# Out-projection of a squared-relu feed-forward as seven block products in place of eight

## The chip, the cores and the metric

The kernel runs on one core of one Trainium2 chip. The metric is the device time of one execution in microseconds (us), and the median over the executions is quoted. All comparisons below use executions of the fast state, unless the text says otherwise. The engines are called TensorE (PE in the profile; PEld is its weight load), VectorE (DVE), ScalarE (ACT), GpSimd (POOL) and SyncE (SP).

## The reference

Sliding-window causal attention (window 64) over 8 batches of 8 heads, 576 positions and 64 columns, then a feed-forward layer with a squared relu over the 4608 tokens. Cut to what matters:

```python
def _attn_ref(q, k, v):                        # (8, 8, 576, 64) each
    scores = np.matmul(q, k.transpose(0, 1, 3, 2)) / np.sqrt(D)
    mask = (rel >= 0) & (rel < 64)             # rel = query position - key position
    ...                                        # softmax over the masked scores
    return np.matmul(attn, v)

def _moe_ref(x, w_in, w_out):                  # (4608, 512), (512, 2048), (2048, 512)
    h = np.maximum(x @ w_in, 0.0)
    return (h * h @ w_out).astype(np.float32)
```

## The kernel before

The 4608 tokens are nine groups of 512. For a group, the attention makes `xT`; the up-projection makes `h2 = relu(x @ w_in)^2` in fp16, 16 slices of 128 features; the out-projection multiplies `h2` by `w_out`. Groups 0 and 1 are special: there the data arrive while the attention is still being computed, so the up-projection goes in chunks of 128 tokens (matmuls of 128 columns). From group 2 on the up-projection uses matmuls of 512 columns and is woven together with the out-projection of the group before and the attention of the group after. A list scheduler fixes the final order of each engine's queue when the kernel is built; where the timelines below show a VectorE op held up, the ops behind it are late as well (e9: one copy of 2.46 us, and the three ops behind it end with it).

The parts that the change touches, and those that the argument needs:

```python
    wst = ctx.enter_context(tc.tile_pool(name="wst", bufs=4))
    stage = ctx.enter_context(tc.tile_pool(name="stage", bufs=15))
    st16 = ctx.enter_context(tc.tile_pool(name="st16", bufs=8))
    hrp = ctx.enter_context(tc.tile_pool(name="hrp", bufs=4))
    opool = ctx.enter_context(tc.tile_pool(name="opool", bufs=4))
    ps_up = ctx.enter_context(tc.tile_pool(name="ps_up", bufs=2, space=bass.MemoryType.PSUM))
    ps_out = ctx.enter_context(tc.tile_pool(name="ps_out", bufs=2, space=bass.MemoryType.PSUM))
    # ... cut ...
    def load_w_out():
        def one(f):
            ws = wst.tile([P, DM], FP32, name="ws2", tag="ws")
            nc.sync.dma_start(out=ws[:], in_=moe_w_out[f * P:(f + 1) * P, :])
            nc.gpsimd.tensor_copy(out=w_out_sb[:, f, :], in_=ws[:])      # fp32 -> fp16 cast

        return [lambda f=f: one(f) for f in range(FFC)]

    def load(i):                       # 128 tokens of k, q, v: DMA, then casts on GpSimd
        # ... cut ...
        nc.gpsimd.tensor_copy(out=k16s[i][:], in_=sts[0][:].rearrange("p h d -> p (h d)"))
        nc.gpsimd.tensor_copy(out=q16s[i][:], in_=sts[1][:].rearrange("p h d -> p (h d)"))
        # ... cut: the same for v, three copies ...

    def scores(i):
        # ... cut: 16 small matmuls, exp on ScalarE ...
            nc.vector.tensor_tensor(out=pm[:], in0=pm[:], in1=mask, op=ALU.min)   # the mask op

    def ffn_up_chunk(i):               # groups 0 and 1
        def one(fq):
            # ... cut: 16 matmuls of 128 columns into one PSUM bank hps ...
            hrelu = hrp.tile([P, 4, P], FP32, name="hrelu4", tag="hrelu")
            nc.scalar.activation(out=hrelu[:], in_=hps[:], func=AF.Relu)
            nc.vector.scalar_tensor_tensor(
                out=h2s[g][:, 4 * fq:4 * fq + 4, t0:t0 + P], in0=hps[:], scalar=0.0,
                in1=hrelu[:], op0=ALU.max, op1=ALU.mult)                # the squared-relu op

    def ffn_out(g):
        hold = {}

        def one(ts, fq):
            if fq == 0:
                hold["ps"] = ps_out.tile([P, DM], FP32, name="ops", tag="ps_o")
            for f in range(4 * fq, 4 * fq + 4):
                nc.tensor.matmul(
                    hold["ps"][:], h2s[g][:, f, ts * P:(ts + 1) * P], w_out_sb[:, f, :],
                    start=(f == 0), stop=(f == FFC - 1))
            if fq == 3:
                osb = opool.tile([P, DM], FP32, name="osb", tag="osb")
                nc.scalar.activation(out=osb[:], in_=hold["ps"][:], func=AF.Copy,
                                     scale=OUT_SCALE)
                # ... cut: DMA of osb to out ...
    # ... cut ...
    for g in range(1, NTB + 1):
        streams = [(ffn_out(g - 1), 0.0, 1.0)]
        if g >= 2 and g < NTB:
            streams.append((ffn_up(g), 0.0, 1.0))
        if g + 1 < NTB:
            streams.append((attention(g + 1), 0.0, 0.85))
        if g + 2 < NTB:
            streams.append((loads(g + 2), 0.0, 1.0))
        for s in weave(*streams):
            s()
```

The softmax here doesn't subtract the row's maximum and nothing guards it: scores larger than these inputs give would overflow.

Of the kernel before, what the change touches and what calls it, by code (L numbers as in the profile page):

```python
# [9 lines left out]
FP32 = mybir.dt.float32  # L10
FP16 = mybir.dt.float16
AF = mybir.ActivationFunctionType
ALU = mybir.AluOpType
# [14 lines left out]
def kernel(  # L28
# [21 lines left out]
    FFC = DFF // P  # L50
    NTB = NT // 512

    const = ctx.enter_context(tc.tile_pool(name="const", bufs=1))
    wst = ctx.enter_context(tc.tile_pool(name="wst", bufs=4))
    stage = ctx.enter_context(tc.tile_pool(name="stage", bufs=15))
    st16 = ctx.enter_context(tc.tile_pool(name="st16", bufs=8))
    attw = ctx.enter_context(tc.tile_pool(name="attw", bufs=3))
    smallp = ctx.enter_context(tc.tile_pool(name="smallp", bufs=4))
    xtp = ctx.enter_context(tc.tile_pool(name="xtp", bufs=3))
    h2pool = ctx.enter_context(tc.tile_pool(name="h2pool", bufs=2))  # L60
    hrp = ctx.enter_context(tc.tile_pool(name="hrp", bufs=4))
    opool = ctx.enter_context(tc.tile_pool(name="opool", bufs=4))
    ps_up = ctx.enter_context(tc.tile_pool(name="ps_up", bufs=2, space=bass.MemoryType.PSUM))
# [45 lines left out]
    def load_w_in():  # L109
# [14 lines left out]
        return steps  # L124

    def load_w_out():
        def one(f):
            ws = wst.tile([P, DM], FP32, name="ws2", tag="ws")
            nc.sync.dma_start(out=ws[:], in_=moe_w_out[f * P:(f + 1) * P, :])
            nc.gpsimd.tensor_copy(out=w_out_sb[:, f, :], in_=ws[:])  # L130

        return [lambda f=f: one(f) for f in range(FFC)]

# [35 lines left out]
    def transposes(i):  # L169
# [10 lines left out]
        nc.vector.tensor_copy(out=kT[:, :, 64:192], in_=ps[:, 0])  # L180
        qT = attw.tile([P, HP, P], FP16, name="qT", tag="qT")
        nc.scalar.activation(out=qT[:], in_=ps[:, 1], func=AF.Copy, scale=1.0)
# [16 lines left out]
    def transpose_q_dma(i):  # L199
        qT = attw.tile([P, HP, P], FP16, name="qTd", tag="qTd", bufs=8)  # L200
        nc.sync.dma_start_transpose(out=qT[:], in_=q16s[i][:])
        qTs[i] = qT
# [49 lines left out]
    def attention(g):  # L252

        steps = []
        fns = (transposes_k, scores, values, to_xT_dma)
        for t in range(4 + len(fns) - 1):
# [5 lines left out]
    def loads(g):  # L262
        steps = []
        for i in range(4 * g, 4 * g + 4):
            steps.append(lambda i=i: load(i))
            if i > 4 * g:
                steps.append(lambda i=i - 1: transpose_q_dma(i))
        steps.append(lambda i=4 * g + 3: transpose_q_dma(i))
        return steps
# [49 lines left out]
    def ffn_out(g):  # L319
        hold = {}  # L320

        def one(ts, fq):
            if fq == 0:
                hold["ps"] = ps_out.tile([P, DM], FP32, name="ops", tag="ps_o")
            for f in range(4 * fq, 4 * fq + 4):
                nc.tensor.matmul(  # L326
                    hold["ps"][:], h2s[g][:, f, ts * P:(ts + 1) * P], w_out_sb[:, f, :],
                    start=(f == 0), stop=(f == FFC - 1))
            if fq == 3:
                osb = opool.tile([P, DM], FP32, name="osb", tag="osb")  # L330
                nc.scalar.activation(out=osb[:], in_=hold["ps"][:], func=AF.Copy,  # L331
                                     scale=OUT_SCALE)
                nc.sync.dma_start(
                    out=out[(g * 4 + ts) * P:(g * 4 + ts + 1) * P, :], in_=osb[:])

        return [lambda ts=ts, fq=fq: one(ts, fq) for ts in range(4) for fq in range(4)]

# [61 lines left out]
```

## Time and profile before

| | before |
|---|---|
| time, median of 3 (range) | 338.17 us (337.17 to 339.39) |
| span of the profiled execution, mean granted TensorE clock | 336.6 us, 0.984 |
| TensorE busy, VectorE busy, GpSimd busy | 314.3, 199.6, 123.2 us |
| end of the last 128-column up-projection | 75.9 us |
| start of the first 512-column up-projection (group 2) | 110.6 us |
| first matmuls of the out-projections of groups 2 to 8 | 120.8, 161.4, 194.6, 226.9, 259.1, 291.1, 318.7 us |

The two middle rows split the program into stages.

The busy time of each engine in two stretches of the kernel before (columns: stretch, length, then busy time and number of instructions of PE, PEld, DVE, ACT and POOL, granted clock, DMA share, GB/s):

```profile
48.00:76.00 28.00, 25.98 (x466) 22.55 (x464) 23.97 (x55) 16.16 (x30) 19.21 (x32) 1.00 1.03 236
...
226.80:259.00 32.20, 32.20 (x275) 15.32 (x273) 20.80 (x48) 15.92 (x28) 9.69 (x16) 1.00 0.52 125
```

The first is the end of the 128-column stage: TensorE 26.0 of 28, VectorE 24.0 of 28. The second is one full iteration of the steady stage: VectorE has 11 us of room in 32.

VectorE's timeline of the kernel before, from 55 us on (start, duration, engine, line, operation, tiles, shapes):

```profile
55.02 0.41 DVE L220 TENSOR_TENSOR pm_1061<-pm_1061,mask_inner 128x512 f16<-128x512 f16 x1
55.40 0.43 DVE L220 TENSOR_TENSOR pm_1064<-pm_1064,mask_inner 128x512 f16<-128x512 f16 x1
55.89 0.69 DVE L306 SCALAR_TENSOR_TENSOR h_1087<-hps_1147,hrelu_1164 128x512 f16<-128x512 f32 x1
```

Two masks and a squared-relu op follow each other within 1.6 us. TensorE's timeline of the kernel before at the two milestones (start, duration, engine, line, operation, tiles, shapes):

```profile
74.86 1.05 PE L301 MATMUL hps_1557<-xT,w_in_sb 128*128 128x128 f16 x16
...
110.61 1.68 PE L280 MATMUL hps<-xT,w_in_sb 128*128 128x512 f16 x7
```

### The profile page before, as it was taken

To read this page: it belongs to the slowest core of one execution; us is meant where nothing else is said; L and a number is where in the kernel's file an instruction comes from. 1 tells how busy PE (TensorE), PEld (TensorE's weight loads), DVE (VectorE), ACT (ScalarE), POOL (GpSimd) and SP (SyncE) were. 2 spreads that over 40 slices of the span, in tenths; PEclk is the share of its full clock that TensorE was granted. 3 is DMA by queue.
4 is the path that set the end of the run, shared out by engine and by line. 5 is a ranking of instruction groups with operands and counts; after the bars stand their busy time and mean duration, and the time that the engine had idled before them with its cause. 6 is when DMAs were issued, how large, how long until landed. Compare 5 with 4: busy or idle time off the path is not lost.

```text
span 336.6 us, 7505 instructions
## 1 busy us (share of the span) xinstructions
PE 314.3 (93%) x2922; PEld 166.6 (49%) x2922; DVE 199.6 (59%) x478; ACT 148.8 (44%) x261; POOL 123.2 (37%) x204
## 2 busy tenths in 40 slices
PE   1957989999999999999999999999999999999995
PEld 0345778884554444444444454444444444444442
DVE  2655888981466687765586478646764666443300
ACT  1123656642333645453454445445543544444411
POOL 5007797586543553553172356337300000000000
PEclk9995899999999999999999999999999999999999
DMA  7899998898977987987793799899622013100121
GB/s 210 248 250 205 207 257 228 246 221 166 217 176 194 238 202 176 247 175 160 177 214 84 178 237 192 142 225 217 137 66 78 33 50 69 38 33 31 40 86 62
DMA packets 152803, 53.97 MB, mean 160 GB/s; under 512 B 144064, under 2 KB 144064, under 8 KB 152768
## 3 DMA queue, kind: packets, MB, share of 16 engines
q1 hardware_dynamic: 152768, 53.50, 68.0%
q8 instruction: 23, 0.38, 0.5%
q14 instruction: 12, 0.10, 0.1%
HBM read 36.70 MB, written 9.44 MB: 137 GB/s over the span
## 4 chain that ended last, share of the span: by engine, by line
PE 78%; DVE 10%; DMA 5%; ACT 3%; issue 1%; SPq 1%; ACTq 0%
PE ops L326 37%; PE hps L280 27%; DMA ws<-in_moe_w_in_dram 5%; PE av L230 4%; PE qkT_ps L189 2%; DVE h_397 L306 1%; DVE h_1087 L306 1%; DVE w_in_sb L117 1%; DVE h_2013 L285 1%; SPq L151 1%; PE hps_639 L301 1%; ACT hrelu L284 1%; DVE x_sb L235 1%; PE hps_506 L301 0%; PE qkT_ps L173 0%
## 5 line engine op out<-in xcount | busy, mean ns | idle before, releaser
L280 PE MATMUL hps<-xT,w_in_sb 128*128 128x512 f16 x448 | 113.2, 379 | 0.9 <-DVE h_3020 L285 0.4
L284 ACT ACTIVATE hrelu<-hps 128x512 f32<-128x512 f32 x112 | 66.9, 597 | 93.6 <-PE hps L280 91.8
L280 PEld LDWEIGHTS <-w_in_sb 128*128 128x128 f16 x448 | 43.3, 98 | 52.4 <-issue 2.1
L301 PEld LDWEIGHTS <-w_in_sb 128*128 128x128 f16 x512 | 32.0, 101 | 7.5 <-issue 2.7
L331 ACT ACTIVATE osb<-ops 128x512 f32<-128x512 f32 x36 | 21.5, 598 | 31.5 <-PE ops L326 30.7
L235 DVE TENSOR_TENSOR x_sb<-av,rden 128x256 f16<-128x256 f32 x72 | 27.5, 415 | 0.1
L285 DVE SCALAR_TENSOR_TENSOR h_4970<-hps,hrelu 128x512 f16<-128x512 f32 x16 | 11.1, 692 | 16.6 <-ACT hrelu L284 16.6
L196 DVE COPY kT<-qkT_ps 128x512 f16<-128x512 f16 x28 | 11.8, 422 | 12.9 <-PE qkT_ps L189 12.8
L234 DVE RECIPROCAL rden<-av 128x4 f32<-128x4 f32 x72 | 10.8, 175 | 13.9 <-PE av L230 13.9
L210 PEld LDWEIGHTS <-kT 64*128 64x128 f16 x576 | 11.5, 96 | 14.7 <-issue 12.6
L326 PE MATMUL ops<-w_out_sb,h_2013 128*128 128x512 f16 x64 | 17.3, 380 | 0.0
L326 PE MATMUL ops<-w_out_sb,h_2515 128*128 128x512 f16 x64 | 16.7, 380 | 0.0
L285 DVE SCALAR_TENSOR_TENSOR h_4528<-hps,hrelu 128x512 f16<-128x512 f32 x16 | 11.1, 692 | 9.4 <-ACT hrelu L284 9.1
L326 PE MATMUL ops<-w_out_sb,h_3522 128*128 128x512 f16 x64 | 16.5, 380 | 0.0
L326 PE MATMUL ops<-w_out_sb,h_3020 128*128 128x512 f16 x64 | 16.5, 380 | 0.0
L326 PE MATMUL ops<-w_out_sb,h_4027 128*128 128x512 f16 x64 | 16.5, 380 | 0.0
L326 PE MATMUL ops<-w_out_sb,h_4528 128*128 128x512 f16 x64 | 16.4, 379 | 0.0
L285 DVE SCALAR_TENSOR_TENSOR h_2515<-hps,hrelu 128x512 f16<-128x512 f32 x16 | 11.0, 688 | 8.6 <-ACT hrelu L284 8.5
L285 DVE SCALAR_TENSOR_TENSOR h_4027<-hps,hrelu 128x512 f16<-128x512 f32 x16 | 11.1, 692 | 8.1 <-ACT hrelu L284 7.9
L285 DVE SCALAR_TENSOR_TENSOR h_3522<-hps,hrelu 128x512 f16<-128x512 f32 x16 | 11.0, 687 | 8.0 <-ACT hrelu L284 7.9
L326 PE MATMUL ops<-w_out_sb,h_1087 128*128 128x512 f16 x64 | 15.7, 380 | 0.0
L285 DVE SCALAR_TENSOR_TENSOR h_3020<-hps,hrelu 128x512 f16<-128x512 f32 x16 | 11.0, 690 | 7.9 <-ACT hrelu L284 7.8
(783 smaller groups left out, 578.1 us busy)
## 6 DMA issues: line engine op xcount, KB each, us to landing
out_dram<-osb SPq DMA_DIRECT2D x36, 256.0 KB, 2.6
k_st<-in_k_dram SPq DMA_DIRECT2D x32, 256.0 KB, 3.7
q_st<-in_q_dram SPq DMA_DIRECT2D x32, 256.0 KB, 4.0
v_st<-in_v_dram SPq DMA_DIRECT2D x32, 256.0 KB, 4.2
ws<-in_moe_w_in_dram SPq DMA_DIRECT2D x16, 256.0 KB, 4.1
k_st<-in_k_dram SPq DMA_DIRECT2D x8, 128.0 KB, 3.4
q_st<-in_q_dram SPq DMA_DIRECT2D x8, 128.0 KB, 3.1
v_st<-in_v_dram SPq DMA_DIRECT2D x8, 128.0 KB, 4.1
```

What stands on the lines that cost most here:

```text
L189: nc.tensor.transpose(out=ps[:, hp, :], in_=src[i][:, hp * P:(hp + 1) * P], identity=ident[:])
L196: nc.vector.tensor_copy(out=kT[:, :, 64:192], in_=ps[:])
L210: nc.tensor.matmul(sc[hh][:, hp, blk, :], kTs[i][r0:r0 + 64, hp, 64 * blk:64 * blk + P], qTs[i][r0:r0 + 64, hp, 64 * blk:64 * blk + 64], s ...
L230: nc.tensor.matmul(av[64 * blk:64 * blk + 64, h % 4, 0:65], pms[i][h % 2][:, h // 2, blk, :], vv[:, h, 0:65], start=True, stop=True)
L234: nc.vector.reciprocal(out=rden[:], in_=av[:, :, 64:65])
L235: nc.vector.tensor_tensor(out=x_sb[:, 4 * half:4 * half + 4, :], in0=av[:, :, 0:D], in1=rden[:].to_broadcast([P, 4, D]), op=ALU.mult)
L280: nc.tensor.matmul(hps[:], w_in_sb[:, c, f * P:(f + 1) * P], xT_of(g)[:, c, :], start=(c == 0), stop=(c == DMC - 1))
L284: nc.scalar.activation(out=hrelu[:], in_=hps[:], func=AF.Relu)
L285: nc.vector.scalar_tensor_tensor(out=h2s[g][:, f, :], in0=hps[:], scalar=0.0, in1=hrelu[:], op0=ALU.max, op1=ALU.mult)
L301: nc.tensor.matmul(hps[:, f, :], w_in_sb[:, c, (4 * fq + f) * P:(4 * fq + f + 1) * P], xT_of(g)[:, c, t0:t0 + P], start=(c == 0), stop=(c ...
L326: nc.tensor.matmul(hold["ps"][:], h2s[g][:, f, ts * P:(ts + 1) * P], w_out_sb[:, f, :], start=(f == 0), stop=(f == FFC - 1))
L331: nc.scalar.activation(out=osb[:], in_=hold["ps"][:], func=AF.Copy, scale=OUT_SCALE)
```

## The change

The out-projection of one group is a product of a 2x2-block matrix (tokens 0 to 255 and 256 to 511, features 0 to 1023 and 1024 to 2047) and a 2x2-block `w_out` (features, output columns). Strassen's form needs seven block products in place of eight, so the intent is to take an eighth of the out-projection off TensorE. It pays with four sums of `h2` blocks per group (fp16, on VectorE, in two halves each: eight ops of 1024 elements per partition), four sums of `w_out` blocks once (16 ops of 512 on GpSimd) and five sums of results per group on VectorE as they leave PSUM. To make room in memory several pools become smaller, and the transposes of q for group 2 move from DMA to TensorE.

```diff
+    GQD = 3
-    stage = ctx.enter_context(tc.tile_pool(name="stage", bufs=15))
-    st16 = ctx.enter_context(tc.tile_pool(name="st16", bufs=8))
+    stage = ctx.enter_context(tc.tile_pool(name="stage", bufs=9))
+    st16 = ctx.enter_context(tc.tile_pool(name="st16", bufs=6))
+    spool = ctx.enter_context(tc.tile_pool(name="spool", bufs=1))
-    hrp = ctx.enter_context(tc.tile_pool(name="hrp", bufs=4))
-    opool = ctx.enter_context(tc.tile_pool(name="opool", bufs=4))
+    hrp = ctx.enter_context(tc.tile_pool(name="hrp", bufs=3))
+    opool = ctx.enter_context(tc.tile_pool(name="opool", bufs=3))
     # ... cut; in load_w_out():
+        def sums(k0):
+            ks, kl = slice(k0, k0 + 2), slice(KH + k0, KH + k0 + 2)
+            b11, b12 = w_out_sb[:, ks, 0:NH], w_out_sb[:, ks, NH:DM]
+            b21, b22 = w_out_sb[:, kl, 0:NH], w_out_sb[:, kl, NH:DM]
+            tt = nc.gpsimd.tensor_tensor
+            tt(out=wb[1][:, ks], in0=b22, in1=b12, op=ALU.subtract)
+            tt(out=b12, in0=b12, in1=b11, op=ALU.subtract)
+            tt(out=wb[0][:, ks], in0=b22, in1=b12, op=ALU.subtract)
+            tt(out=wb[2][:, ks], in0=b21, in1=wb[0][:, ks], op=ALU.subtract)
+        steps = []
+        for k in range(KH):
+            steps += [lambda f=k: one(f), lambda f=KH + k: one(f)]
+            if k % 2 == 1:
+                steps.append(lambda k0=k - 1: sums(k0))
     # ... cut; in ffn_out(g), for the old body:
+        S = [spool.tile([P, KH, TH], FP16, name=f"hs{i}", tag=f"hs{i}") for i in range(4)]
+        def hsum(i, half):
+            ks = slice(half * KH // 2, (half + 1) * KH // 2)
+            x, y, op = ((A[1][0], A[1][1], ALU.add), (S[0], A[0][0], ALU.subtract),
+                        (A[0][0], A[1][0], ALU.subtract), (A[0][1], S[1], ALU.subtract))[i]
+            nc.vector.tensor_tensor(out=S[i][:, ks], in0=x[:, ks], in1=y[:, ks], op=op)
+        # ... cut: product() issues 16 matmuls of 256 columns per half; evac() empties a bank,
+        #     ScalarE for a plain copy, VectorE (scale, then add) where a sum is due
+        plan = [
+            ("A", A[0][0], W[0][0], True, (("A", "p1"),)),
+            ("B", S[1], wb[0], True, (("B", "u2", "p1"),)),
+            ("A", A[0][1], W[1][0], False, (("A", "osb", None, 0, 0),)),
+            ("C", S[0], W[0][1], True, (("C", "u4", "u2"),)),
+            ("D", S[2], wb[1], True, (("D", "osb", "u4", 1, 1),)),
+            ("C", S[3], W[1][1], False, (("C", "osb", "u2", 0, 1, True),)),
+            ("D", A[1][1], wb[2], False, (("D", "osb", "u2", 1, 0, True),)),
+        ]
+        before = {0: (0, 1), 2: (2,), 4: (3,)}
```

More of the change, by code (lines that the diff above doesn't have):

```diff
@@ L124, in load_w_in @@
         return steps
+    KH = FFC // 2
+    NH = DM // 2
+    wb = [const.tile([P, KH, NH], FP16, name=f"wb{i}") for i in range(3)]
     def load_w_out():
@@ L130, in one @@
             nc.gpsimd.tensor_copy(out=w_out_sb[:, f, :], in_=ws[:])
-        return [lambda f=f: one(f) for f in range(FFC)]
+        def sums(k0):
[12 more added lines that the diff above has]
+                steps.append(lambda k0=k - 1: sums(k0))
+        return steps
     xTs = {}
@@ L180, in transposes @@
         nc.vector.tensor_copy(out=kT[:, :, 64:192], in_=ps[:, 0])
-        qT = attw.tile([P, HP, P], FP16, name="qT", tag="qT")
+        qT = attw.tile([P, HP, P], FP16, name="qT", tag="qT", bufs=8)
         nc.scalar.activation(out=qT[:], in_=ps[:, 1], func=AF.Copy, scale=1.0)
@@ L199, in transpose_q_dma @@
     def transpose_q_dma(i):
-        qT = attw.tile([P, HP, P], FP16, name="qTd", tag="qTd", bufs=8)
+        qT = attw.tile([P, HP, P], FP16, name="qT", tag="qT", bufs=8)
         nc.sync.dma_start_transpose(out=qT[:], in_=q16s[i][:])
@@ L254, in attention @@
         steps = []
-        fns = (transposes_k, scores, values, to_xT_dma)
+        fns = (transposes_k if g >= GQD else transposes, scores, values, to_xT_dma)
         for t in range(4 + len(fns) - 1):
@@ L265, in loads @@
             steps.append(lambda i=i: load(i))
-            if i > 4 * g:
+            if g >= GQD and i > 4 * g:
                 steps.append(lambda i=i - 1: transpose_q_dma(i))
-        steps.append(lambda i=4 * g + 3: transpose_q_dma(i))
+        if g >= GQD:
+            steps.append(lambda i=4 * g + 3: transpose_q_dma(i))
         return steps
@@ L319, in ffn_out @@
     def ffn_out(g):
-        hold = {}
-        def one(ts, fq):
-            if fq == 0:
-                hold["ps"] = ps_out.tile([P, DM], FP32, name="ops", tag="ps_o")
-            for f in range(4 * fq, 4 * fq + 4):
-                nc.tensor.matmul(
-                    hold["ps"][:], h2s[g][:, f, ts * P:(ts + 1) * P], w_out_sb[:, f, :],
-                    start=(f == 0), stop=(f == FFC - 1))
-            if fq == 3:
-                osb = opool.tile([P, DM], FP32, name="osb", tag="osb")
-                nc.scalar.activation(out=osb[:], in_=hold["ps"][:], func=AF.Copy,
-                                     scale=OUT_SCALE)
-                nc.sync.dma_start(
-                    out=out[(g * 4 + ts) * P:(g * 4 + ts + 1) * P, :], in_=osb[:])
@@ L336, in ffn_out @@
-        return [lambda ts=ts, fq=fq: one(ts, fq) for ts in range(4) for fq in range(4)]
+        h2 = h2s[g]
+        TH = 256
+        top = (slice(0, TH), slice(0, KH)), (slice(0, TH), slice(KH, FFC))
+        bot = (slice(TH, 512), slice(0, KH)), (slice(TH, 512), slice(KH, FFC))
+        A = [[h2[:, ks, ts] for ts, ks in row] for row in (top, bot)]
+        S = [spool.tile([P, KH, TH], FP16, name=f"hs{i}", tag=f"hs{i}") for i in range(4)]
+        banks, sums, osb = {}, {}, {}
+        def hsum(i, half):
[3 more added lines that the diff above has]
+            nc.vector.tensor_tensor(out=S[i][:, ks], in0=x[:, ks], in1=y[:, ks], op=op)
@@ new lines, in product @@
+        def product(bank, a, w, half, first):
+            if first and half == 0:
+                banks[bank] = ps_out.tile([P, 2, NH], FP32, name=f"ops{bank}", tag="ps_o")
+            for k in range(half * KH // 2, (half + 1) * KH // 2):
+                for m in range(2):
+                    nc.tensor.matmul(
+                        banks[bank][:, m, :], a[:, k, m * P:(m + 1) * P], w[:, k],
+                        start=(first and k == 0 and m == 0), stop=(k == KH - 1),
+                        skip_group_check=True)
@@ new lines, in evac @@
+        def evac(bank, to, add=None, row=0, col=0, send=False):
+            if to == "osb":
+                if row not in osb:
+                    osb[row] = opool.tile([P, 2, DM], FP32, name="osb", tag="osb")
+                dst = osb[row][:, :, col * NH:(col + 1) * NH]
+            else:
+                sums[to] = wst.tile([P, 2, NH], FP32, name=to, tag="ws")
+                dst = sums[to][:]
+            if add is None:
+                nc.scalar.activation(out=dst, in_=banks[bank][:], func=AF.Copy, scale=OUT_SCALE)
+            else:
+                nc.vector.scalar_tensor_tensor(
+                    out=dst, in0=banks[bank][:], scalar=OUT_SCALE, in1=sums[add][:],
+                    op0=ALU.mult, op1=ALU.add)
+            if send:
+                r0 = g * 512 + row * TH
+                nc.sync.dma_start(
+                    out=out[r0:r0 + TH, :].rearrange("(m p) d -> p m d", p=P), in_=osb[row][:])
@@ new lines, in ffn_out @@
+        W = [[w_out_sb[:, 0:KH, 0:NH], w_out_sb[:, 0:KH, NH:DM]],
+             [w_out_sb[:, KH:FFC, 0:NH], w_out_sb[:, KH:FFC, NH:DM]]]
+        plan = [
[7 more added lines that the diff above has]
+        ]
@@ new lines, in ffn_out, with step @@
+        before = {0: (0, 1), 2: (2,), 4: (3,)}
+        steps = []
+        for n, (bank, a, w, first, evs) in enumerate(plan):
+            for half in range(2):
+                def step(n=n, bank=bank, a=a, w=w, first=first, evs=evs, half=half):
+                    for i in before.get(n, ()):
+                        hsum(i, half)
+                    product(bank, a, w, half, first)
+                    if half == 1:
+                        for e in evs:
+                            evac(*e)
+                steps.append(step)
@@ L341 @@
+        return steps
     load(0)
```

## The prediction

> **What bounds the kernel now.** TensorE, from about 75 us on. The page has PE busy 93% of the span; pace says more: in the timeline 64 matmuls of 512 columns take 13.8 us, 216 ns each. The first matmuls of successive groups' out-projections are 32.2, 32.2 and 32.0 us apart (one full iteration); two projections are 27.65 us of that, attention 4.5. The chain of waits gives the two projections 64%. Before 75 us it is mixed: DMA share 0.8 to 1.0, VectorE about 88% busy (windows, 50 to 70 us).
>
> **What the change does, per group of 512 tokens (nine).**
> - TensorE: 64 matmuls x 512 columns become 112 x 256. The 128-column matmuls run 16 in 1.05 us, 56 ns apart with weight loads hidden; I estimate 109 ns per 256 columns: 12.2 us for 13.8. Saves 1.6 us, 14.6 over nine.
> - VectorE adds eight fp16 sums of 1024 elements. A mask op of 512 repeats every 0.35 us; estimate 0.62 each, 4.9 us. It adds five PSUM combines at 0.61 us (spacing of the squared-relu op), 3.1 us. ScalarE loses two copies.
> - A full iteration has 19.9 us of VectorE without GpSimd work; the mask ops take 3.5 us at 9.7 us of GpSimd work and 4.8 at 15.0. The Trainium skill, "SBUF — State Buffer" (Who interferes with whom), says a VectorE op with two SBUF inputs and a GpSimd op that reads SBUF block each other; the trace agrees (mask 0.41 us, often 0.83 beside GpSimd). The sums are of this kind. So VectorE goes to about 28 us without GpSimd and 30 to 32 with, against a TensorE need of 30.5: co-bottleneck in four of five full iterations.
> - GpSimd adds 16 weight sums of 512. "GPSIMD Engine Reference" (Performance versus the Vector engine) measures about 2.6 cycles per element for two inputs; estimate 1.1 us each, 18 us, from 50 us on, where its casts leave about 6.5 us idle. Casts from chunk 9 on slip some 12 us (first from 71 to about 83); TensorE wants it near 82.
> - Staging falls from 15 to 9 buffers; group 2's q-transposes move from DMA to TensorE.
>
> **Critical path.** Group 2's first up-projection starts at 110.4 us now. TensorE saves 3.2 us before it; later casts and a fuller VectorE take it back: 109 to 113 after. Then 17 us to the next projection, five full iterations at 30.5 if TensorE binds and about 32 where VectorE does, one without attention at 26.0 (now 27.6), the last at 14.2 (12.2 plus waits for sums and a bank; now 13.8), 5 of drain (now 4.3). Span about 332, 1.6 more as time. Of 14.6 us saved, about 4 survive.
>
> **Prediction: 334 us, 8 in 10 within 324 to 345. Faster by over 2%: 0.30; within 2%: 0.58; slower: 0.12.**
>
> **What would show it.** Right: out-projection matmuls 109 ns apart; VectorE busy from 200 to about 272 us, over 27 per full iteration; full iterations 31 to 33 us with GpSimd work, about 30.5 without; TensorE waits released by VectorE; sums 0.7 us alone, over 1 beside GpSimd; weight sums done near 80 us. Wrong: full iterations at 30.5 throughout (about 327), or matmuls wider than 115 ns.
>
> **What would make it wrong.** Faster: contention costs less, or early-scheduled sums hide it. Slower: in-order VectorE delays the squared-relu op so that TensorE, with two up-projection banks, stalls each step; starvation by shallower staging at 80 to 110 us; sums at one element per cycle, which makes VectorE the plain bound at about 35 us per iteration.

## More of the kernel before

The profile page of the kernel before, its first two parts (busy time of each engine; then busy tenths in 40 slices of 8.4 us):

```profile
PE 314.3 (93%) x2922; PEld 166.6 (49%) x2922; DVE 199.6 (59%) x478; ACT 148.8 (44%) x261; POOL 123.2 (37%) x204
...
PE   1957989999999999999999999999999999999995
...
DVE  2655888981466687765586478646764666443300
...
POOL 5007797586543553553172356337300000000000
```

TensorE is full from the seventh slice (about 50 us) to the end. VectorE has 40% of idle time on average, but its row also shows where it has none: slices 5 to 9, about 34 to 76 us, are 8 and 9 tenths.

## The result, and the profile after

The changed kernel is right and slower: 349.85 us, median of 4 (347.91 to 350.98), against 338.21 (337.17 to 339.39) for the kernel before on the same chip. The ratio is 1.0337, 95% interval 1.0279 to 1.0395. A ratio is the mean time of one kernel's fast runs over the mean of the other's in the same rounds, so it is not quite the ratio of the medians quoted beside it.

| | before | after |
|---|---|---|
| span, granted clock | 336.6 us, 0.984 | 349.2 us, 0.956 |
| end of the last 128-column up-projection | 75.9 | 89.8 |
| first 512-column up-projection (group 2) | 110.6 | 129.0 |
| from there to the end | 226.0 | 220.2 |
| first matmuls of the out-projections of groups 2 to 8 | 120.8, 161.4, 194.6, 226.9, 259.1, 291.1, 318.7 | 146.3, 182.4, 214.7, 245.6, 276.3, 306.8, 331.9 |

The table is the whole result in small: from group 2's first up-projection on, the changed kernel is 5.8 us quicker, and it gets there 18.4 us later. 18.4 − 5.8 is the 12.6 us between the spans. Some 14 of the 18 us are lost already before the end of the 128-column stage.

The profile page of the changed kernel, the same rows (a slice is 8.7 us here):

```profile
PE 310.0 (89%) x3370; PEld 214.9 (62%) x3370; DVE 274.2 (78%) x595; ACT 140.1 (40%) x247; POOL 149.4 (43%) x220
...
PE   1857976769979879999999999999999999999994
...
DVE  2556889897498486997898899979988987975852
...
POOL 4008889999993305636542733723660000000000
```

TensorE's row has holes in slices 6 to 9 (44 to 79 us) and again in 12, 14 and 15 that were not there. GpSimd's row is solid nines in slices 7 to 12, from 52 to 105 us. VectorE is well filled in the steady stage, and TensorE keeps its nines there: the extra VectorE work of the steady stage does not show as holes.

The busy time of the changed kernel in the same stretch, and in a full iteration (columns as before):

```profile
48.00:76.00 28.00, 19.29 (x331) 16.82 (x330) 26.66 (x47) 12.54 (x24) 27.20 (x31) 0.88 0.65 187
...
182.40:214.70 32.30, 32.14 (x328) 20.54 (x326) 28.79 (x65) 15.23 (x27) 14.00 (x22) 1.00 0.81 186
...
245.60:276.30 30.70, 30.70 (x322) 19.94 (x321) 28.01 (x63) 14.45 (x26) 10.12 (x16) 1.00 0.63 146
276.30:306.80 30.50, 30.50 (x318) 19.75 (x317) 26.27 (x60) 14.45 (x26) 0.00 (x0) 1.00 0.17 53
```

In the first row VectorE is busy 26.7 of 28 us, 2.7 more than before, yet with 47 instructions in place of 55: each takes longer. GpSimd goes from 19.2 to 27.2 us, nearly all of the stretch, and TensorE loses 6.7 us. TensorE's granted clock falls too, from 1.00 to 0.88: sixteen 128-column matmuls at 62.8 us took 1.91 us in place of 1.05. From the spacing of these matmuls I estimate that the lower clock cost about 2 us of the stage; it comes together with the waits and was not tested apart from them. In the iterations below TensorE is full, and the later two are shorter than the 32.2 of before.

VectorE's timeline of the changed kernel, where the masks of 55 us were:

```profile
56.18 2.65 DVE L358 TENSOR_TENSOR hs_1651<-h_403 128x1024 f16<-128x1024 f16 x2
58.76 0.82 DVE L245 TENSOR_TENSOR pm_1083<-pm_1083,mask_inner 128x512 f16<-128x512 f16 x1
59.50 1.64 DVE L358 TENSOR_TENSOR hs_1652<-hs_1651,h_403 128x1024 f16<-128x1024 f16 x1
61.06 0.82 DVE L245 TENSOR_TENSOR pm_1086<-pm_1086,mask_inner 128x512 f16<-128x512 f16 x1
61.81 0.68 DVE L332 SCALAR_TENSOR_TENSOR h_1109<-hps_1110,hrelu_1127 128x512 f16<-128x512 f32 x1
```

Three sums of `h2` of group 0 stand in front of and between two masks of group 1's attention. They took 2.65 us for two and 1.64 for one, where the same op later took 0.68; the masks took 0.82. What had been 1.6 us is now 6.3 us, and an up-projection of group 1 waits behind it. Nothing needs these sums yet: the first product that uses `hs_1652` starts at 90.1 us. GpSimd's timeline of the changed kernel shows what ran beside them:

```profile
53.78 1.15 POOL L147 TENSOR_TENSOR wb_150<-w_out_sb 128x512 f16<-128x512 f16 x1
55.02 1.16 POOL L148 TENSOR_TENSOR w_out_sb<-w_out_sb 128x512 f16<-128x512 f16 x1
56.11 0.61 POOL L185 CAST k_1605<-k_st 128x512 f16<-128x512 f32 x1
56.69 1.60 POOL L149 TENSOR_TENSOR wb_149<-w_out_sb 128x512 f16<-128x512 f16 x1
58.23 1.07 POOL L140 CAST w_out_sb<-ws_420 128x512 f16<-128x512 f32 x1
59.27 1.32 POOL L150 TENSOR_TENSOR wb_151<-w_out_sb,wb_149 128x512 f16<-128x512 f16 x1
```

The weight sums run back to back with the casts from 53.8 us on, and both are stretched too (a sum 1.15 to 1.60, a cast 0.61 to 1.07). The Trainium skill, "SBUF — State Buffer" (Who interferes with whom), says that a VectorE op with two SBUF inputs and a GpSimd op that reads SBUF contend; the trace agrees, at 0.68 against 1.04 to 1.64 us for the sums and 0.41 against 0.82 for the masks.

The longest waits of TensorE in the changed kernel between 48 and 90 us (engine, line, releaser: total, times, longest, us; the two lines are one wait, of the weight load and of its matmul):

```profile
PEld L255 <- DVE pm_1083 L245: 2.7, 1, 2.7
PE av L255 <- DVE pm_1083 L245: 2.5, 1, 2.5
```

Its longest wait is for the very mask at 58.76 that stood behind the two sums. Over the whole 128-column stage from 48 us on, TensorE's weight loads waited 11.0 us for masks, against 1.6 us in the kernel before, and only 1.0 us for squared-relu ops, against 1.2. No wait that the profile shows for TensorE there ended with a GpSimd op, so the weight sums did not hold TensorE directly. The timeline of TensorE and the chain of waits of the changed kernel at the milestones:

```profile
88.76 1.07 PE L327 MATMUL hps_1579<-xT,w_in_sb 128*128 128x128 f16 x16
...
129.03 1.44 PE L306 MATMUL hps<-xT,w_in_sb 128*128 128x512 f16 x3 [1.06 <-DMA out_dram<-osb]
```

```profile
111.98 1.75 PE opsA L365 x16
113.73 1.75 PE opsC L365 x16
```

Sixteen matmuls of 256 columns take 1.75 us, 109 ns each: the pace of TensorE was as predicted. (The name of the transfer in the brackets is the profile's guess: that matmul reads `xT`, which arrives by DMA.)

### The profile page after: what moved, and what is told of

The parts are those of the page before. It is cut to its first block, busy times and chain, and to the rows that moved or that the text cites. A ratio compares the mean times of both kernels' runs of the same rounds, so it can differ in the third digit from the quotient of the medians.

```text
span 349.2 us, 8488 instructions
## 1 busy us (share of the span) xinstructions
PE 310.0 (89%) x3370; PEld 214.9 (62%) x3370; DVE 274.2 (78%) x595; ACT 140.1 (40%) x247; POOL 149.4 (43%) x220
## 4 chain that ended last, share of the span: by engine, by line
PE 54%; DVE 10%; ACT 2%; DMA 1%; issue 1%; ACTq 0%
PE hps L306 24%; PE opsD L365 7%; PE opsC L365 7%; PE opsA L365 7%; PE opsB L365 4%; PE av L255 2%; DVE h_2117 L311 2%; ACT hrelu L310 1%; PE qkT_ps L214 1%; DMA out_dram<-osb 1%; DVE h_3248 L311 1%; DVE h_2681 L311 1%; DVE h_3812 L311 1%; DVE osb L381 1%; DVE x_sb L260 0%
## 5 line engine op out<-in xcount | busy, mean ns | idle before, releaser
L306 PE MATMUL hps<-xT,w_in_sb 128*128 128x512 f16 x448 | 115.0, 386 | 2.2 <-DMA out_dram<-osb 1.1
L235 PEld LDWEIGHTS <-kT 64*128 64x128 f16 x576 | 12.4, 98 | 11.0 <-issue 8.9
L119 DVE TENSOR_SCALAR w_in_sb<-ws 128x512 f16<-128x512 f32 x16 | 7.2, 448 | 13.6 <-DMA ws<-in_moe_w_in_dram 13.6
L311 DVE SCALAR_TENSOR_TENSOR h_5446<-hps,hrelu 128x512 f16<-128x512 f32 x16 | 11.0, 689 | 7.4 <-ACT hrelu L310 7.4
L311 DVE SCALAR_TENSOR_TENSOR h_2117<-hps,hrelu 128x512 f16<-128x512 f32 x16 | 10.9, 684 | 4.8 <-ACT hrelu L310 4.5
L207 ACT ACTIVATE qT<-qkT_ps 128x512 f16<-128x512 f16 x12 | 7.1, 595 | 17.0 <-DVE kT L205 16.8
L311 DVE SCALAR_TENSOR_TENSOR h_2681<-hps,hrelu 128x512 f16<-128x512 f32 x16 | 11.0, 685 | 3.4 <-ACT hrelu L310 3.2
L311 DVE SCALAR_TENSOR_TENSOR h_4942<-hps,hrelu 128x512 f16<-128x512 f32 x16 | 11.0, 689 | 2.5 <-ACT hrelu L310 2.3
L311 DVE SCALAR_TENSOR_TENSOR h_3248<-hps,hrelu 128x512 f16<-128x512 f32 x16 | 10.9, 684 | 2.3 <-ACT hrelu L310 2.2
L311 DVE SCALAR_TENSOR_TENSOR h_3812<-hps,hrelu 128x512 f16<-128x512 f32 x16 | 11.0, 685 | 1.7 <-ACT hrelu L310 1.5
L311 DVE SCALAR_TENSOR_TENSOR h_4379<-hps,hrelu 128x512 f16<-128x512 f32 x16 | 10.9, 683 | 1.6 <-ACT hrelu L310 1.5
L221 DVE COPY kT<-qkT_ps 128x512 f16<-128x512 f16 x24 | 9.9, 413 | 1.8 <-PE qkT_ps L214 1.8
L259 DVE RECIPROCAL rden<-av 128x4 f32<-128x4 f32 x72 | 9.9, 167 | 1.1 <-PE av L255 0.7
L342 PE MATMUL warm<-mask_inner,ident 128*128 128x512 f16 x26 | 8.1, 450 | 2.3 <-DVE mask_inner L89 2.3
L379 ACT ACTIVATE osb<-opsA 128x512 f32<-128x512 f32 x9 | 5.4, 597 | 11.2 <-PE opsA L365 11.2
L218 DVE COPY kT<-kT 128x256 f16<-128x256 f16 x24 | 7.4, 309 | 0.2
L205 DVE COPY kT<-qkT_ps 128x512 f16<-128x512 f16 x12 | 5.0, 417 | 2.1 <-PE qkT_ps L198 2.0
```

What stands on the lines that cost most here:

```text
L119: nc.vector.tensor_scalar(out=w_in_sb[:, c, quar * FQ:(quar + 1) * FQ], in0=ws[:], scalar1=W_SCALE, scalar2=None, op0=ALU.mult)
L218: nc.vector.tensor_copy(out=kT[:, :, 0:64], in_=kTs[i - 1][:, :, P:192])
L221: nc.vector.tensor_copy(out=kT[:, :, 64:192], in_=ps[:])
L235: nc.tensor.matmul(sc[hh][:, hp, blk, :], kTs[i][r0:r0 + 64, hp, 64 * blk:64 * blk + P], qTs[i][r0:r0 + 64, hp, 64 * blk:64 * blk + 64], s ...
L259: nc.vector.reciprocal(out=rden[:], in_=av[:, :, 64:65])
L306: nc.tensor.matmul(hps[:], w_in_sb[:, c, f * P:(f + 1) * P], xT_of(g)[:, c, :], start=(c == 0), stop=(c == DMC - 1))
```

## The experiments

The question: where did the 18 us before group 2 come from? Four suspects, all in the first 130 us: the weight sums on GpSimd, the sums of `h2` of groups 0 and 1 on VectorE, the two together (each blocks the other), and the smaller pools. All experiments were timed in turn with the kernel before on the same chip. Medians are those of the fast runs: one run each of e1 (755.78 us), e2 (339.21) and e7 (348.00) was slow and is left out here, while the expectations quote medians over all runs. The three milestones at the right come from one profiled execution of each kernel; the spans of a kernel's fast executions differ by 1 to 4 us, so differences of a microsecond between milestones say little. This table has the numbers; the texts follow. (A chunk is 128 tokens; group 2's second chunk is "chunk 9" in the expectations.)

| run | output | ratio to before (95%) | median us, fast runs | 128-column stage ends | first 512-column up-projection | first k cast of group 2's second chunk |
|---|---|---|---|---|---|---|
| before | right | 1 | 338.2 | 75.9 | 110.6 | 71.0 |
| changed kernel | right | 1.0337 (1.0279 to 1.0395) | 349.85 | 89.8 | 129.0 | 86.4 |
| e1: no weight sums | wrong | 1.0019 (0.997 to 1.0067) | 338.51 | no usable profile | | |
| e6: the same kernel again | wrong | 1.0073 (1.0017 to 1.0128) | 340.46 | 82.5 | 118.2 | 69.7 |
| e2: no `h2` sums in groups 0, 1 | wrong | 0.996 (0.9896 to 1.0025) | 335.03 | 75.0 | 112.3 | 80.5 |
| e5: neither | wrong | 0.9815 (0.9771 to 0.9859) | 331.89 | 75.6 | 111.4 | 69.8 |
| e3: before + weight sums | right | 1.0225 (1.0177 to 1.0272) | 345.3 | 78.7 | 117.2 | 82.5 |
| e4: before + smaller pools | right | 0.9992 (0.9951 to 1.0033) | 337.95 | 76.9 | 111.4 | 69.8 |
| e7: `h2` sums of group 0 held | right | 1.0148 (1.0088 to 1.0208) | 342.20 | 79.5 | 122.2 | 86.9 |
| e10: weight sums on VectorE | right | 1.0198 (1.0148 to 1.0249) | 344.83 | 86.5 | 122.8 | 71.1 |
| e9: memsets for weight sums | wrong | 1.0168 (1.0101 to 1.0236) | 344.31 | 84.0 | 123.0 | 80.5 |
| e12: tiny copies for weight sums | wrong | 1.0115 (1.0068 to 1.0163) | 342.03 | 81.5 | 120.8 | 83.5 |
| e8: eight products in groups 0, 1 | right | 0.9861 (0.9826 to 0.9896) | 333.31 | 78.0 | 112.0 | 69.8 |
| e11: e8, weight sums held | right | 0.9801 (0.9752 to 0.985) | 331.31 | 75.1 | 109.9 | 67.9 |

### e1 and e6: the changed kernel without weight sums

The products then use plain blocks of `w_out`, so the output is wrong; everything else stays.

```diff
-            if k % 2 == 1:
-                steps.append(lambda k0=k - 1: sums(k0))
+        wb = (W[1][1], W[0][1], W[1][0])       # in ffn_out
```

> The changed kernel without the 16 weight sums on GpSimd; the products take plain weight blocks instead, so the output is wrong on purpose, and everything else stays. Read already: the full iterations behave as predicted (30.5 to 32.3 us); the 19 us are lost before the first up-projection of group 2, which starts at about 129 us instead of 110.4. Theory GpSimd (the weight sums, 20 us of GpSimd work, make the casts late and stretch VectorE's two-input work): that start comes back to 109 to 114, GpSimd is no longer busy without a break from 48 to 98 us, and the time is 331 to 337. Theory VectorE (sums of h2 of groups 0 and 1 in the start): start at 124 or later, time 344 to 350. Theory staging: the same as VectorE, 344 to 350.

The fast runs were 336.84, 338.51 and 340.16 us: ratio 1.0019. The profiled execution was an outlier of 755.78 us, TensorE shown busy throughout, and of no use; the same kernel was therefore run again for its profile.

> The same kernel as the first run without weight sums, whose profile fell in an execution of 755 us and says nothing. Wanted is a profile of a normal execution, at 337 to 341 us. Contention: the h2 sums of groups 0 and 1 take about 0.7 us each instead of 1.05 to 1.64, the last 128-column up-projection ends at 79 to 84 (89.8 with the weight sums), group 2's up-projection starts at 115 to 119. Independent costs: sums still at about 1.2 us.

Ratio 1.0073. So taking the weight sums away recovers most of the loss (3.4 − 0.2 to 0.7 points), but not all of it: 337 us was the upper edge of what the theory of GpSimd alone allowed. The 128-column stage still ends at 82.5 us, 6.6 later than before.

### e2: the changed kernel without the h2 sums of groups 0 and 1

```diff
+        if g < 2:
+            before = {}
+            S = [A[1][0], A[0][0], A[0][0], A[0][1]]
```

> The changed kernel with the sums of h2 left out for groups 0 and 1 only (plain blocks go into those products; output wrong on purpose); the weight sums stay on GpSimd. Theory VectorE: the last 128-column up-projection of group 1 ends near 77 us again (89.8 in the changed kernel), group 2's up-projection starts by 114, time 332 to 338. Theory GpSimd: it helps only by the contention that it takes away, 2 to 6 us: time 344 to 348, start at 123 to 127. Theory staging: within 2 us of the changed kernel's 349.9.

Median 335.03, ratio 0.996, with the weight sums on GpSimd all there and GpSimd as full (27.4 us busy of 48 to 76). The 128-column stage ends at 75.0 us. This speaks for VectorE's queue as the place; but GpSimd's sums were also nearly enough by themselves to make the loss (e1). Either removal looks like the cure, which says that the two are not separate costs. Hence e5.

### e5: neither

> Both left out: no weight sums on GpSimd, no sums of h2 for groups 0 and 1 (output wrong on purpose). It is the fourth corner of a square with the changed kernel (349.9), no weight sums (339.3) and no h2 sums in groups 0 and 1 (335.2). Theory of independent costs: the two savings of 10.5 and 14.7 add up, giving 324 to 327. Theory of contention (each op that is added makes the other kind longer, so either removal takes away the shared part as well): 329 to 334, with group 2's up-projection starting at 107 to 111 us.

The edits of e1 and e2 together. Ratio 0.9815. The four cells, in points of the time before:

| | no weight sums | weight sums on GpSimd |
|---|---|---|
| no `h2` sums in groups 0, 1 | −1.85 | −0.4 |
| `h2` sums in groups 0, 1 | +0.2 and +0.7 | +3.4 |

From the first cell, the weight sums alone cost 1.45 points (5 us) and the `h2` sums alone 2.0 to 2.6 (7 to 9 us). Both cost 5.2 points, 18 us: 1.2 to 1.7 points, 4 to 6 us, more than the two added. So the costs do not look independent, as expected of contention. Each ratio is known to about half a point, so the extra is known to about a point (an estimate from the four intervals) and only just clears the noise; e12 below is the stronger evidence.

### e3: the kernel before with the weight sums added, unused

```diff
+    wb = [const.tile([P, KH, NH], FP16, name=f"wb{i}") for i in range(4)]
+            tt = nc.gpsimd.tensor_tensor       # the four sums, b12-b11 into wb[3]; w_out stays
-    stage = ctx.enter_context(tc.tile_pool(name="stage", bufs=15))
+    stage = ctx.enter_context(tc.tile_pool(name="stage", bufs=12))   # room for wb
```

> The kernel before with the 16 weight sums added on GpSimd (written to tiles of their own that nobody reads, same order of weight loads as in the changed kernel; staging 12 buffers instead of 15 to make room). Output right. Theory GpSimd: that alone moves group 2's first up-projection from 110.4 to 120 to 127 us and the time to 348 to 355. Theory VectorE or staging: it costs under 4 us, time 338 to 342.

345.3 us, between the two expectations: +7 us. There are no `h2` sums here, so I read it as GpSimd's lateness and its blocking of the masks; the two were not separated. It is more than the 5 us of e2 against e5. One difference is that here q of group 2 is transposed by DMA after its cast; that this makes a late cast dearer was not tested and stays open.

### e4: the kernel before with the smaller pools

```diff
-    stage ... bufs=15    -    st16 ... bufs=8    -    hrp ... bufs=4
+    stage ... bufs=9     +    st16 ... bufs=6    +    hrp ... bufs=3
```

> The kernel before with only the buffer counts of the change: 9 staging tiles for 15, 6 fp16 tiles for 8, 3 relu tiles for 4. Output right. Theory staging (shallow prefetch starves the first groups): time 346 to 352, group 2's up-projection at 119 or later. The other two theories: within 2 us of before, 336 to 340.

Ratio 0.9992. The theory of the smaller pools falls. The edit leaves out two more differences of the change, three output tiles in place of four and q of group 2 transposed on TensorE. Both are in e5 as well, which reaches group 2 at 111.4 us, so they are not what costs the 18 us.

### e7: the h2 sums of group 0 held back

A one-column copy from the last piece of group 1's `h2` into every sum tile makes the sums of group 0 wait until the 128-column stage is over. The copy is overwritten, and the output is right.

```diff
+        if g == 0:
+            for t in S:
+                for k in (0, KH // 2):
+                    nc.vector.tensor_copy(out=t[:, k, 0:1], in_=h2s[1][:, FFC - 1, 511:512])
```

> The changed kernel, output right, with one thing moved: the sums of h2 of group 0 are held in VectorE's order behind the last squared-relu of group 1 (eight one-column copies give the dependency), so none of them stands among the first two groups' up-projections. The weight sums stay on GpSimd. If the loss is VectorE's in-order queue (sums that nobody needs yet stand before squared-relus that TensorE waits for, at 1.05 to 1.64 us each[...]): the last 128-column up-projection ends at 75 to 79 us instead of 89.8, and the time is 336 to 342. If the loss is GpSimd's late casts: that end may move, but group 2's up-projection still starts at 124 or later and the time is 345 or more.

The 128-column stage ends at 79.5 us, 10.3 earlier than in the changed kernel, so it was the sums' place in VectorE's queue that held it up. But the time falls by only 1.9 points, about 6.4 us, with fast runs of 341.57, 342.20 and 345.22: the eight sums now run from 81.4 to 86.3 us, and TensorE's weight loads for the products wait 2.9 us for them once, before the first 512-column up-projection at 122.2. Moving the sums moves the wait; it does not remove it. Stage end and time lie just above the ranges of the first theory, and below the time of the second, so neither number held.

The held sums also had an effect that was not expected. GpSimd's timeline in e7, then VectorE's:

```profile
81.42 5.39 POOL L192 COPY v_od<-v_ev 64x512 f16<-64x512 f16 x1
```

```profile
81.44 1.28 DVE L362 TENSOR_TENSOR hs<-h 128x1024 f16<-128x1024 f16 x2
...
85.05 1.29 DVE L362 TENSOR_TENSOR hs<-h,hs 128x1024 f16<-128x1024 f16 x2
```

While the eight sums ran without a pause, at 0.68 to 0.69 us each, a GpSimd copy of a kind that took 0.61 us at 88.66 in the same run took 5.39. The first k cast of group 2's second chunk stands right behind it, at 86.9. Here it is GpSimd that paid.

### e10: the weight sums on VectorE

```diff
-            tt = nc.gpsimd.tensor_tensor
+            tt = nc.vector.tensor_tensor
```

> The changed kernel with its 16 weight sums on VectorE in place of GpSimd; the output is right. VectorE gets about 16 x 0.4 us = 6.4 us more before 90 us, GpSimd loses 21 to 23 us there and its casts are back at about 70 us. Theory BLOCKING: less is lost than by the sums on GpSimd although VectorE, already the fullest engine there, now does more: up-projections end at 83 to 87, time 341 to 346. Theory PLAIN VECTOR LOAD (only VectorE's added time counts): 6 us more of it than in the kernel without weight sums (339 to 340), so up-projections end at 88 to 90 and the time is 346 to 350.

Ratio 1.0198, 344.83 us, stage end 86.5 us. VectorE has the work of both and is busy for all of 76 to 90 us, and still this is 3 us earlier than with the sums on GpSimd. The expectation of contention (341 to 346) held, near its upper edge.

### e9: memsets in place of the weight sums

This and e12 were to part two readings of the weight sums: GpSimd's queue is late, so its casts come late, or its sums and VectorE's block each other. GpSimd was kept as busy with something that was meant not to contend.

```diff
-            tt(...)                                    # four sums
+            for i, b in ((0, b22), (1, b22), (2, b21)):   # keeps the place behind the casts
+                nc.gpsimd.tensor_copy(out=wb[i][:, ks, 0:1], in_=b[:, :, 0:1])
+            for i in (1, 1, 0, 0, 0, 0, 2, 2):
+                nc.gpsimd.memset(wb[i][:, ks], 1.0)
```

> The changed kernel, but each of the 16 weight sums on GpSimd is replaced by two memsets of 512 fp16 elements into the weight-sum tiles (they write and read nothing; a memset of 128 elements took 0.21 us and one of 64 took 0.15, so I estimate about 0.53 us for 512 and 1.06 for the pair, nearly the 1.15 to 1.60 of a sum), behind a tiny copy that keeps their place. The products read plain blocks of w_out, so the output is wrong on purpose. GpSimd stays about as busy and its casts about as late (first cast of chunk 9 at 82 to 86 us, against 69.7 with no weight sums and 86.4 in the changed kernel). Theory LATE CASTS (the weight sums cost time because GpSimd's own queue falls behind): 347 to 351 us, like the changed kernel, 128-column up-projections ending at 87 to 90. Theory BLOCKING (the two-input sums of GpSimd and VectorE stop each other): the h2 sums of groups 0 and 1 come back to 0.7 to 0.9 us, the up-projections end at 81 to 84, and the time is 339 to 343, like the kernel with no weight sums at all.

344.31 us: between the theories, and the trace shows that the control was not clean. GpSimd's timeline in e9, then VectorE's:

```profile
53.00 3.79 POOL L148 MEMSET wb<- 128x512 f16 x8
```

```profile
54.41 2.46 DVE L200 COPY kT<-kT 128x256 f16<-128x256 f16 x1
54.54 2.33 DVE L356 TENSOR_TENSOR hs<-h 128x1024 f16<-128x1024 f16 x2
55.74 1.13 DVE L243 TENSOR_TENSOR pm<-pm,mask_inner 128x512 f16<-128x512 f16 x1
```

All three VectorE lines end at about 56.87, just after the burst of memsets ends (53.00 + 3.79 = 56.79). The fast copy of `kT` (0.22 us when nothing is in its way) waited the burst out, and the two others stand behind it. Two more bursts show the same (copies of 1.38 and 3.58 us, each ending 0.1 us after its burst). The Trainium skill, "SBUF — State Buffer" (Who interferes with whom), says that copies between SBUF tiles can enter a fast mode of VectorE that contends with GpSimd, and that the loser waits for the whole instruction; the wait here was longer than that, several instructions of about 0.5 us.

### e12: tiny copies in place of the weight sums

```diff
-            tt(...)                                    # four sums
+            for j in range(32):
+                nc.gpsimd.tensor_copy(out=wb[j % 3][:, ks, j:j + 1],
+                                      in_=(b21, b22)[j % 2][:, :, j:j + 1])
```

> The changed kernel, each group of four weight sums on GpSimd replaced by 32 copies of 128x2 elements in the same place (such a copy took about 0.15 us in the run with memsets, three in 0.44, so I estimate 4.7 us for 32, nearly the 5 to 5.7 of four sums); they keep GpSimd's queue as long but move almost no data. Output wrong on purpose. The memsets were no clean control: a fast fp16 copy of kT on VectorE (128x256, SBUF to SBUF) waited out whole bursts of eight memsets, 2.5 and 3.6 us. First cast of chunk 9 at 80 to 86 us in either case. Theory LATE CASTS: 346 to 350 us as in the changed kernel. Theory BLOCKING: sums of h2 and masks as short as with no weight sums at all (eight sums 6.5 to 7.5 us together, 10.3 in the changed kernel), 128-column up-projections ending at 81 to 84 us (82.5 with no weight sums, 89.8 in the changed kernel) and a time of 339 to 343, a little above the run with no weight sums for the later casts. If a VectorE op is again seen waiting for a whole burst, the control has failed again and the run only bounds the answer.

342.03 us, stage end 81.5: the values of blocking, not of late casts. GpSimd's queue was as full and as late as in the changed kernel: busy time in e12 in the same stretch, and GpSimd's timeline:

```profile
48.00:76.00 28.00, 23.06 (x408) 20.24 (x408) 26.75 (x57) 14.44 (x27) 27.62 (x115) 0.94 0.61 175
```

```profile
52.98 5.93 POOL L146 COPY wb<-w_out_sb 128x2 f16<-128x2 f16 x32
```

VectorE's timeline in e12 beside that burst:

```profile
55.31 0.22 DVE L199 COPY kT<-kT 128x256 f16<-128x256 f16 x1
55.44 1.29 DVE L355 TENSOR_TENSOR hs<-h 128x1024 f16<-128x1024 f16 x2
56.64 0.42 DVE L242 TENSOR_TENSOR pm<-pm,mask_inner 128x512 f16<-128x512 f16 x1
56.98 0.68 DVE L355 TENSOR_TENSOR hs<-hs,h 128x1024 f16<-128x1024 f16 x1
57.58 0.42 DVE L242 TENSOR_TENSOR pm<-pm,mask_inner 128x512 f16<-128x512 f16 x1
```

The three sums and two masks that took 5.7 us in the changed kernel (56.18 to 61.88) take 2.6 us. The first eight sums took 5.9 us together against 10.3; the eight masks between 48 and 80 us 0.52 each against 0.96 (0.54 in the kernel before). One impurity remains: a `kT` copy at 66.93 took 2.46 us and ended with a run of four casts, and the bursts delay the casts, so that fewer casts run beside VectorE in this stage, which would favour this run: its stage ends 1.0 us before that of e6, which has no weight sums and no copies. How large that is was not measured.

A rival would be that the scheduler built another order for each kernel. The traces rule it out on VectorE: up to the last squared-relu op of group 1, its order in the changed kernel, in e6 and in e12 is the same but for two `kT` copies near the end. And the waits of TensorE's weight loads for masks in this stage go with the stage ends: 1.7 us in e5, 3.1 in e12, 5.8 in e6, 11.0 in the changed kernel.

### e8 and e11: seven products from group 2 on only

If the price is paid in groups 0 and 1 and the gain comes in the others, keep eight products for the first two groups. The weight sums are then wanted only when group 2's out-projection begins, and go to VectorE. In e11 they are also held, by the one-column copy of e7, behind the last squared-relu op of group 1.

```diff
+    GS = 2                                    # and GQD = 2: q of group 2 by DMA, as before
+        return ffn_out7(g) if g >= GS else ffn_out8(g)
+            tt = nc.vector.tensor_tensor      # own tile for b12-b11, w_out stays as it is
+            for w in wb:                      # e11 only, ahead of each four sums
+                nc.vector.tensor_copy(out=w[:, k0, 0:1], in_=h2s[1][:, FFC - 1, 511:512])
```

> A version meant to win, output right: groups 0 and 1 by the eight products of before, groups 2 to 8 by seven; the 16 weight sums are on VectorE (0.35 us each) instead of GpSimd (1.15 to 1.6); group 2's q-transposes on the DMA as before; buffer counts of the change. If the loss is all in the start: group 2's up-projection starts at 110 to 114 as before, the rest takes 219 to 221, time 330 to 335. If the seven products also cost in the full iterations in some way that the trace did not show: 337 or more.

> The version with eight products in groups 0 and 1 and seven in the other seven groups, weight sums on VectorE; now the weight sums are held behind the last squared-relu op of group 1 by a one-column copy from it into each weight-sum tile. Output right. The 128-column up-projections should end at about 76 us (78.0 without the hold, 75.9 in the kernel before); if those 2 us count, the time is 330 to 333 (333.3 without the hold); if the wait for the attention of group 2 behind it takes them back, it stays 332.5 to 334.5.

e8: 333.31 us, ratio 0.9861. The scheduler still placed some of the weight sums among the last 128-column up-projections (stage end 78.0). With the hold in e11 the stage ends at 75.1 and group 2 starts at 109.9: 331.31 us, ratio 0.9801 (0.9752 to 0.985), right, and the fastest version. It is as fast as e5 (331.89), which has no weight sums and no `h2` sums in groups 0 and 1 and computes a wrong result. The page of e11:

```profile
PE 304.1 (92%) x3258; PEld 199.4 (61%) x3258; DVE 261.3 (79%) x601; ACT 139.1 (42%) x247; POOL 128.4 (39%) x204
...
POOL 5008897576734474364146357147700000000000
```

## Why the prediction was wrong

Point by point, in the order of the prediction:

- **TensorE's pace: right.** 109 ns per 256-column matmul, as estimated.
- **VectorE's added work: right in sum.** 274.2 us busy against "about 272"; an `h2` sum 0.68 alone and 1.04 to 1.64 beside GpSimd, as "0.7 alone, over 1 beside".
- **TensorE waits released by VectorE: right**, but in the 128-column stage (2.7 us for one mask, 11.0 in all), not in the full iterations. Among its risks the prediction named an in-order VectorE that delays the squared-relu op; the ops that TensorE waited for were the masks.
- **Full iterations: nearly right.** Predicted 31 to 33 with GpSimd work and 30.5 without. The five were 36.1, 32.3, 30.9, 30.7 and 30.5; the counterpart of the first took 40.6 in the kernel before. VectorE needed 26 to 29 us in the last four, not 28 to 32, so it stayed just under TensorE. The stretch from group 2's first up-projection to the end came to 220.2 us, where the prediction's terms add up to about 221. That this agrees to a microsecond is partly luck: the first iteration was 4 us over its term, and later terms and the end about 5 under. The gain that it promised for the steady stage is there.
- **The smaller pools: right to leave out** (e4, ratio 0.9992; e5 for what e4 leaves out).
- **Weight sums "done near 80 us", "casts slip some 12 us": too low, but by little.** They were done at 85.7, and the cast slipped by 15.4.
- **The failed step: "Group 2's first up-projection starts at 110.4 us now. TensorE saves 3.2 us before it; later casts and a fuller VectorE take it back: 109 to 113 after."** It came at 129.0. With 129.0 in place of 111 the prediction's own sum for the span, 332, becomes 350; the profile has 349.2.

What was overlooked is in the prediction's own readings. It noted that VectorE was about 88% busy from 50 to 70 us, that the weight sums would fill GpSimd from 50 us on, and that the two kinds of sum block each other. It costed the `h2` sums one by one in the full iterations only, where VectorE had 11 us of room; for the stretch before group 2 it allowed 2 to 6 us for "later casts and a fuller VectorE" together, without a sum. But the scheduler put the sums of group 0 as early as their inputs allowed, into a stage where VectorE had 4 us of room in 28 and GpSimd had just become full.

The 17.6 us between e5 (neither) and the changed kernel, at the start of group 2, can be split by the milestones of the runs:

| step | from, to | us |
|---|---|---|
| `h2` sums early in VectorE's queue | stage end 75.6 (e5) to 82.5 (e6) | 6.9 |
| GpSimd's queue kept full, without blocking | 82.5 (e6) to 81.5 (e12) | −1.0 |
| two-input sums on both engines at once | 81.5 (e12) to 89.8 (changed) | 8.3 |
| not settled: late casts, or a result combine late in VectorE's queue | stage end to group 2's start, 35.8 (e5) to 39.2 (changed; 39.3 in e12) | 3.4 |

The first three lines are shown by the runs, to some 2 us: each milestone is that of one execution, and e12 is not quite pure. The last is shown only as a difference. It goes with late casts: the stretch is 35.7 to 36.2 us where the cast came by 71.1 (e5, e6, e10) and 39.0 to 39.3 in e9, e12 and the changed kernel, though 37.3 in e2, with the cast 10.7 us late. But TensorE's longest idle time in it, 2.1 us in the changed kernel and 2.4 in e12 (a like wait is 0.6 in e5 and 1.1 in e6), ends with a result combine on VectorE that stood in its queue behind `h2` sums of group 1 and masks. How the late casts lead to that, or whether they do, stays open. The times agree in order: e5 to e6 costs 2.6 points of the time before, e6 to e12 0.4, e12 to the changed kernel 2.2.

A part of the promise also failed for e5: TensorE's 3.2 us of saving before group 2 did not bring its start forward (111.4 against 110.6 before) even without any sums. In that stretch the new order puts group 2's attention behind blocks of products, and the transposes of its q are on TensorE; neither was tried alone, and why the saving does not come through stays open.

## What to carry to other kernels

Work that an idle engine "has room for" has to be placed in time before it is costed: ask into which stage the scheduler may pull it, and read the busy share of that stage, not the average of the span. When a change gives two engines work of the same kind at the same moment, count what each does to the other; either half alone cost 5 to 9 us and the two cost 18. Where a gain is spread over all groups and the price is paid in the first ones, keep the old form in those: here that turned 3.4% slower into 2.0% faster.

## What the Trainium skill lacked or had wrong

- "SBUF — State Buffer" (Who interferes with whom): that two-input VectorE ops contend with GpSimd ops that read SBUF agrees (in the changed kernel sums 0.68 to 1.64 us, masks 0.41 to 1.37). It lacks that a fast VectorE copy can be held for a whole run of GpSimd instructions, not one: 2.46 and 3.58 us behind bursts of eight memsets of about 0.5 us each (e9), and 2.46 us to the end of a run of four casts (e12). Nor does it say that a GpSimd copy can be held for a whole run of VectorE's two-input ops: 5.39 us in place of 0.61, beside eight sums (e7).
- The same section has no size for what such contention costs a kernel: 8.3 us at the end of the 128-column stage here (e12 to the changed kernel), with both engines nearly full.
- "GPSIMD Engine Reference" (Performance versus the Vector engine): about 2.6 cycles per element for two inputs led to an estimate of 1.1 us per weight sum of 512; measured 1.14 at best and up to 1.60 beside VectorE, 4 to 45% above the estimate.
- "TensorE: Matmul & The Clock Gate" (Back-to-back issue gap) gives sustained figures of about 131 ns per matmul of 512 columns and 81 ns per matmul of 128 for a stream with weight loads. In this kernel, with a weight load for each matmul, 512 columns take 216 ns and 128 columns about 56; 256 columns take 109. These fit the section's formula for the isolated gap, which it says under-counts at 128 columns and over-counts at 512 in a stream.
- No page has the price of work that a scheduler places early in an in-order queue: eight sums of 0.68 to 1.12 us among the up-projections moved the end of the stage by 6.9 us (e5 to e6), with GpSimd hardly fuller (22.5 against 21.1 us of 28).
